# Gated expert values made during attention, the down projection as seven products of blocks, and a transposed result

## The chip, the cores and the metric

The kernel runs on one core of one Trainium2 chip. The metric is the time of one execution on the device in microseconds (us); lower is better. The median of three runs of the kernel before is 1683.87 us (1683.67 to 1683.97).

## The reference

One input x of S = 2048 tokens and D = 512 goes through softmax attention (H = 32 heads of 16) and through a gated expert (F = 1792), and a gate per token mixes the two:

```python
g = sigmoid((x * gate_w).sum(-1, keepdims=True))
q, k, v = split(x @ wqkv)                     # 32 heads of 16
a = softmax(q @ k.T * 16 ** -0.5) @ v @ wo    # per head, heads joined before wo
h = sigmoid(x @ w_gate) * (x @ w_up)          # 2048 x 1792
b = h @ w_down
return g * a + (1 - g) * b
```

Everything is float32. The kernel keeps that precision on TensorE by writing each operand as a high part and a low rest (fp32r) and adding three matmuls for one product: high x high, high x low, low x high.

## The kernel before

**Words used here.** PE is TensorE, ACT ScalarE, DVE VectorE, POOL GpSimd; SP's queue starts the DMAs. P = 128 rows; a chunk c is 512 of the 2048 tokens; f counts the 14 row blocks of 128 of the hidden size. `split` (ends in L104) makes the high part by a copy on ACT (L101) and the low rest by a subtraction on DVE or POOL. Work on PE, ACT, DVE and POOL runs in the order in which the code emits it; SP's DMAs are put where what they need is ready.

**Attention** is a loop over 256 periods `k`, each for two blocks of keys. In a period PE makes eight scores for the maxima (L292; DVE reduces each, L294), eight scores for the exponentials (L679; ACT, L681), twelve half-height matmuls of other dense work (L162: the gate and up projections, the projections of queries and keys, then the first heads), and at its end sixteen matmuls of the values (L842), whose 128x512 sum ACT copies (`part`, L847) and POOL adds (`sum`, L859). The string `STEADY` gives the order of these, `spot` the bank of each. After every 32 steps of keys, in each eighth period (k mod 8 = 4), DVE transposes the maxima (L298, L300) and POOL splits them (L319). The word `turn` is a token: an empty POOL instruction that waits for PE's half-height matmuls on one half of the array, and that the matmuls of the other half wait for. It stands in POOL's row among POOL's other work.

POOL's work comes from queues (`later`, `turnover`, `slow`), from which `work(2.0)` and `work(2.6)` take entries twice per period by an estimated cost: the sums (`sum`), the combinations of the dense products (`chain`, `had`, `side`, L542), and the splits of weights (`ca`, `cb`, L139 and L136). In periods 75 to 122 DVE also computes the gate's logits (L829, sixteen in all). From period 245 on (`FREE`) no maxima are left and the order `LAST` is used.

The gate and up projections go to `gu_d` in DRAM, as gate and up before the sigmoid. In the last 16 periods the hidden values of the first two pairs of blocks are made (`hidden_early`: exponentials on ACT, L768, and reciprocals on DVE, L776).

**The tail** has 28 rounds (c, two blocks f), each of 24 down matmuls (L1034), with a chunk's four token blocks in four banks. For each round ahead of PE a 512 KB load of gate and up comes in, ACT applies the sigmoid (L759), DVE multiplies (L760), ACT and DVE split the product (L101, L104). ACT and POOL split the rest of `w_down` and `wo` in the first rounds. The heads' values are multiplied by the reciprocal denominators (L987, from `rec_d`), split, and multiplied by `wo` (L149) in eight places between the rounds; `finish` (L1002, L1006) scales with the gate, a column of one number per token, adds, and stores rows of tokens. The denominators' reciprocals are L800.

Of the kernel before, what the change touches and what calls it, by code (L numbers as in the profile page):

```python
# [25 lines left out]
P = 128  # L26
KT = D // P
# [12 lines left out]
EARLY = 5  # L40
# [6 lines left out]
def gated_mix(ctx, tc, x, xT, wqk, wv, wo, w_gate, w_up, w_down, gate_w, out):  # L47
# [26 lines left out]
    hp_d = dram.tile([2 * EARLY, P, D], F32, name="hp_d")  # L74
# [122 lines left out]
    xes = ExitStack()  # L197
    xp = xes.enter_context(tc.tile_pool(name="xp", bufs=1))
# [123 lines left out]
    wd = []  # L322

# [64 lines left out]
    def filling():  # L388
# [5 lines left out]
        jobs += [("heads", 0), ("down", 0)]  # L394
# [5 lines left out]
        def raws(kind, n):  # L400
# [9 lines left out]
            if kind == "down":  # L410
                return [raw_weights(w_down[f * P:(f + 1) * P, :], [P, D], f"wd{f}") for f in range(2)]
# [8 lines left out]
        def weights(kind, n, loaded):  # L420
# [4 lines left out]
            if kind in ("heads", "down"):  # L425
                return [split_weights(r) for r in loaded]
# [49 lines left out]
        def sums_of(kind, n, ws):  # L476
# [29 lines left out]
            elif kind == "heads":  # L506
                for u in range(EARLY):
                    while split_of[u] in later:
                        later.pop(0)[1]()
                    oh, ol = [t for t in first_heads(u)][:2]  # L510
                    for a in range(2):
                        cols = slice(a * P, (a + 1) * P)
                        run = Sum(bankd(), [((oh[:, k, cols], ol[:, k, cols]), ws[k]) for k in range(2)])
                        yield run
                        sp.dma_start(hp_d[2 * u + a], out_of(run, f"hp{u}_{a}"))
# [54 lines left out]
        for job, nxt in zip(jobs, jobs[1:]):  # L570
            kind, n = job
            coming = None
            for at, run in enumerate(sums_of(kind, n, ws)):
# [13 lines left out]
                if kind == "heads" and at in (2, 4, 6):  # L587
                    if at == 2:
                        first_heads_load(4)
                    first_heads_split(at // 2 + 1)  # L590
                if at == ask[kind][0]:
                    coming = raws(*nxt)
                if at == ask[kind][1]:
                    new = weights(*nxt, coming)
                    end = turnover[-1]
# [9 lines left out]
        wd.extend(ws)  # L605
# [106 lines left out]
    chunks = [(c, f) for c in range(NC) for f in range(0, NF, 2)]  # L712

    def hidden_load(c, f):
        gu = big(f"gul{c}_{f}").rearrange("p (a f s) -> p a f s", a=2, f=2)
        for a in range(2):
            sp.dma_start(gu[:, a], gu_d[a, f:f + 2, :, c * 512:(c + 1) * 512].rearrange("f p s -> p f s"))
        return gu

    def late_raw(src, r):  # L720
        if src is w_down and r in (6, 8):
            raw = [keep.tile([P, D], F32, name=f"late{r + a}", tag="er", bufs=6) for a in range(2)]
            for a in range(2):
                sp.dma_start(raw[a], src[(r + a) * P:(r + a + 1) * P, :])
            return raw
        raw = keep.tile([P, 2, D], F32, name=f"late{r}", tag="ev", bufs=2)
        sp.dma_start(raw, src[r * P:(r + 2) * P, :].rearrange("(k p) d -> p k d", p=P))
        return raw

    def down_late(f, raw):  # L730
        if f < 6:
            th, tl, bufs = ("wh", "wl", 4) if f < 4 else ("sum", "part", 2)
            for a in range(2):
                if f + a == 5:
                    th = tl = "wr"
                h = keep.tile([P, D], F32R, name=f"wd{f + a}h", tag=th, bufs=bufs)
                l = keep.tile([P, D], F32R, name=f"wd{f + a}l", tag=tl, bufs=bufs)
                split(h, l, raw[:, a, :], act, pool)
                wd.append((h, l))
        else:  # L740
            fs = slice(f - 6, f - 4)
            if f < 10:
                for a in range(2):
                    split(wd_h[:, f - 6 + a, :], wd_l[:, f - 6 + a, :], raw[a], act, pool)
# [157 lines left out]
    for k in range(NPER):  # L902
# [27 lines left out]
        if k == NPER - 1:  # L930
            break
# [157 lines left out]
```

## Time and profile before

| | |
|---|---|
| median of the runs | 1683.87 us |
| span of the profiled execution | 1682.4 us |
| PE busy | 1677.3 us (100%) |
| DVE busy | 1451.8 us (86%) |
| ACT busy | 1362.8 us (81%) |
| POOL busy | 941.9 us (56%) |
| bytes moved by DMA | 254.20 MB |
| first down matmul to the last | 1493.87 to 1678.5 us |

The profile is of one execution. "Busy" counts the time in which an engine had an instruction running. A row of an engine in order of time reads: start, duration (both us), engine, line, operation, output <- input, shape, number of instructions, and in brackets how long the engine sat idle before it and what released it. A group's row has the sum of the busy time and the mean of one in ns, then idle time by releaser. A row with "x16" covers sixteen instructions that follow each other.

### The profile page before, as it was taken

The numbers are of one execution on the slowest core, as the hardware profiler recorded it, in microseconds if no ns is written. First come the engines' busy times: TensorE is split into PE (matmuls) and PEld (weight loads), VectorE is DVE, ScalarE is ACT, GpSimd is POOL, SyncE is SP. The second block draws the span as 40 slices with busy tenths as digits, with TensorE's granted clock in tenths as the row PEclk, the third lists the DMA queues.
The fourth block names the chain that finished last, engine by engine and source line by source line (L and its number), as shares of the span: only waits on it lengthen the run. The fifth ranks groups of instructions, "written<-read, shape, count | busy, mean of one in ns | idle before, by whom it ended". The sixth has DMA issues, their size and how long they took to land.

```text
span 1682.4 us, 34644 instructions
## 1 busy us (share of the span) xinstructions
PE 1677.3 (100%) x12485; PEld 1063.3 (63%) x12485; DVE 1451.8 (86%) x2347; ACT 1362.8 (81%) x2659; POOL 941.9 (56%) x922
## 2 busy tenths in 40 slices
PE   9999999999999999999999999999999999999999
PEld 7766566665656565656565666656565656568887
DVE  7988888888889999999888888888999888887853
ACT  4188898989888898889898989898898989983431
POOL 1034476547666666666666767676766667653110
PEclk9999999999999999999999999999999999999999
DMA  7511457356565564566635353534353534368861
GB/s 247 140 48 59 128 175 210 134 164 209 143 199 133 167 153 157 159 165 184 166 102 146 102 145 108 134 103 133 107 137 104 133 115 153 128 205 277 294 211 70
DMA packets 143788, 254.20 MB, mean 151 GB/s; under 512 B 24256, under 2 KB 36544, under 8 KB 140736
## 3 DMA queue, kind: packets, MB, share of 16 engines
q1 hardware_dynamic: 136000, 237.30, 47.1%
q10 hardware_dynamic: 7616, 14.68, 2.8%
q8 instruction: 98, 1.61, 0.4%
q14 instruction: 74, 0.61, 0.2%
HBM read 149.42 MB, written 102.50 MB: 150 GB/s over the span
## 4 chain that ended last, share of the span: by engine, by line
PE 97%; DVE 3%; issue 0%; DVEq 0%
PE dn L162 29%; PE sm L842 27%; PE sm L292 15%; PE sm L1034 5%; PE st L679 5%; PE sm L679 4%; PE st L292 2%; DVE stat L294 2%; PE dn L1034 2%; PE st L1034 2%; PE st L643 1%; PE st L149 1%; PE sm L149 1%; PE st L162 1%; PE st L842 1%; PE st L85 0%
## 5 line engine op out<-in xcount | busy, mean ns | idle before, releaser
L294 DVE TENSOR_REDUCE stat<-sm 128x1 f32<-128x512 f32 x1313 | 847.9, 681 | 140.4 <-PE sm L679 126.5
L681 ACT ACTIVATE p<-st 128x512 f32<-128x512 f32 x1019 | 619.2, 655 | 1.1 <-PE st L679 1.1
L681 ACT ACTIVATE p<-sm 128x512 f32<-128x512 f32 x1027 | 611.1, 632 | 0.5 <-PE sm L679 0.2
L292 PE MATMUL sm<-ks,qs 48*128 48x512 f32 x1313 | 522.6, 436 | 0.3
L842 PE MATMUL sm<-p,v 128*17 128x512 f32 x4016 | 480.0, 595 | 0.0
L294 DVE TENSOR_REDUCE stat<-st 128x1 f32<-128x512 f32 x735 | 479.5, 680 | 0.1
L679 PE MATMUL sm<-qs,ks 64*128 64x512 f32 x1027 | 427.6, 419 | 0.0
L679 PE MATMUL st<-qs,ks 64*128 64x512 f32 x1019 | 426.5, 419 | 0.0
L292 PEld LDWEIGHTS sm<-ks,qs 48*128 48x128 f32 x1313 | 239.6, 184 | 259.3 <-DVE stat L294 212.3
L859 POOL TENSOR_TENSOR sum<-sum,part 128x512 f32<-128x512 f32 x224 | 288.6, 1288 | 135.7 <-PE sm L679 118.4
L292 PE MATMUL st<-ks,qs 48*128 48x512 f32 x735 | 290.5, 395 | 0.0
L842 PEld LDWEIGHTS sm<-p,v 128*17 128x17 f32 x4016 | 93.2, 97 | 224.2 <-issue 155.1
L847 ACT ACTIVATE part<-sm 128x512 f32<-128x512 f32 x214 | 128.2, 599 | 124.4 <-issue 83.8
L542 POOL TENSOR_TENSOR chain<-chain,chain 128x512 f32<-128x512 f32 x96 | 124.1, 1292 | 156.3 <-PE sm L679 139.5
L679 PEld LDWEIGHTS st<-qs,ks 64*128 64x128 f32 x1019 | 187.7, 184 | 30.0 <-issue 3.4
L679 PEld LDWEIGHTS sm<-qs,ks 64*128 64x128 f32 x1027 | 189.6, 185 | 9.9 <-issue 5.1
L542 POOL TENSOR_TENSOR had<-chain,had 128x512 f32<-128x512 f32 x96 | 123.5, 1287 | 39.3 <-PE sm L679 20.3
L292 PEld LDWEIGHTS st<-ks,qs 48*128 48x128 f32 x735 | 137.3, 187 | 2.1 <-ACT v L662 0.3
L607 ACT ACTIVATE chain<-dn 128x512 f32<-128x512 f32 x128 | 89.2, 697 | 0.0
L542 POOL TENSOR_TENSOR side<-side,side 128x512 f32<-128x512 f32 x32 | 41.3, 1292 | 76.5 <-PE sm L679 66.1
L104 POOL TENSOR_TENSOR ol<-ot,oh 128x512 fp32r<-128x512 f32 (+1 forms) x8 | 14.7, 1840 | 102.5 <-ACT oh L101 102.5
L319 POOL CAST mhl<-mt 128x32 fp32r<-128x32 f32 x32 | 7.5, 236 | 102.7 <-DVE mt L300 102.7
(913 smaller groups left out, 3253.5 us busy)
## 6 DMA issues: line engine op xcount, KB each, us to landing
gul<-gu_d SPq DMA_DIRECT2D x56, 512.0 KB
had<-gu_d SPq DMA_DIRECT2D x84, 256.0 KB
gu_d<-had SPq DMA_DIRECT2D x84, 256.0 KB
gu_d<-side SPq DMA_DIRECT2D x56, 256.0 KB
pv_d<-sum SPq DMA_DIRECT2D x32, 256.0 KB
qs<-q_d SPq DMA_DIRECT2D x30, 256.0 KB
ks<-k_d SPq DMA_DIRECT2D x30, 256.0 KB
gu_d<-far SPq DMA_DIRECT2D x28, 256.0 KB
```

What stands on the lines that cost most here:

```text
L149: pe.matmul(o, a, b, start=(i == 0), stop=(i == len(ops) - 1))
L162: mm = pe.matmul(self.o, a[rows], b[rows], start=(self.n == 0), stop=(self.n == 2 * len(self.ops) - 1))
L292: pe.matmul(t, qs[r:r + KM, qt * P:(qt + 1) * P], ks[r:r + KM, g * 512:(g + 1) * 512], start=True, stop=True)
L294: dve.tensor_reduce(stat[half][:, b, qt % 8, g:g + 1], t, axis=AX.X, op=ALU.max)
L542: pool.tensor_tensor(to, u, w, ALU.add)
L607: leave = lambda e, o: act.activation(e, o, AF.Copy)
L679: pe.matmul(o, ks[r:r + KR, (kt + a) * P:(kt + a + 1) * P], qs[r:r + KR, q0:q0 + 512], start=True, stop=True)
L681: act.activation(pt[:, 2 * a + c, :], o, AF.Exp, scale=DH ** -0.5)
L842: pe.matmul(o[32 * c:32 * c + VW, :], v[:, 2 * k % 16 + a, h * VW:(h + 1) * VW], pts[c // 2][:, 2 * a + c % 2, :], start=(a == 0), stop=(a ...
L847: act.activation(e, o, AF.Copy)
L859: pool.tensor_tensor(s, s, e, ALU.add)
L1034: pe.matmul(down[t], a, b, start=(f == 0 and m == 0), stop=(f == NF - 2 and m == 5))
```

## The change

**Hidden values.** They are made during attention now. In periods 143 to 249 thirteen "quads" go through: four blocks of a block row pair (i, i + 7) and a chunk pair (c, c + 2). Each of the four has two loads of 256 KB (gate and up), a tanh in two pieces of 128x256 on ACT, one per period, ahead of the values matmuls, and one scalar_tensor_tensor (tanh + 1) * up on DVE, 128x512, right behind the values matmuls of every second period. POOL forms four differences of the four blocks (`quad_steps`, L737), through the queue `later`. The seven operands of each quad, 128x512, are stored to `op_d`. The fourteenth quad is made in the tail (`last_quad`). The factor 1/2 of sigmoid(g) = (tanh(g/2) + 1)/2 goes into the gate's factor g0.

**Down projection.** Hidden values and `w_down` are cut into two by two blocks (of tokens and of F against F and output columns), and each half of the tokens takes seven products in place of eight (A11, A12, A22, S1, S2, S4, S3), each of 7 blocks f x 2 x 3 matmuls. The weights are the stationary operand, so the result is transposed: 128 output columns x 512 tokens. `op_load` and `op_split` bring one operand each, four ahead of PE by the code; `after` adds the products up on DVE. The weight blocks for the first two products are split on DVE in the last periods (`first_weights`); those for the other five are made in the tail by seven calls of `w_split`, with four POOL additions each. The operand tiles of the first four come from tag w, the others from three tiles of two.

**Gate and heads.** The gate's factor is a row now: g0 and g1 go through `g_d` in DRAM and come back broadcast over partitions; g1 is multiplied into the reciprocal denominators (one more DVE operation for each), g0 into the sums on POOL (`scaled`). The early heads are ten transposed half sums (`hp_d`), added on POOL (`plus`). The denominators' reciprocals stand in periods 144 to 215 and, for the second half, at operands 18 to 36 of the tail. The host transposes the result. A scratch size for DMA is set to 1024.

On DVE, at the transposition of maxima in a period with k mod 8 = 4, the rows of before (`stat` are the maxima, `mpad` and `mt` the transposition):

```order
L294 TENSOR_REDUCE stat_0_11201<-sm_71 128x1
L294 TENSOR_REDUCE stat_0_11201<-sm_72 128x1 x2
L294 TENSOR_REDUCE stat_0_11201<-st_65 128x1
L294 TENSOR_REDUCE stat_0_11201<-st_67 128x1
L294 TENSOR_REDUCE stat_0_11201<-sm_72 128x1
```

and of after, in a period with the transposition and in the second one behind it:

```order
L294 TENSOR_REDUCE stat_0_11247<-sm_72 128x1
L298 TENSOR_REDUCE mpad_95<-stat_0_11247 128x16
L300 STREAM_TRANSPOSE mt_0_11793<-mpad_95 128x32
L745 SCALAR_TENSOR_TENSOR hu_11605<-hg_11533,hu_11605 128x512
L294 TENSOR_REDUCE stat_1_11824<-sm_72 128x1
...
L294 TENSOR_REDUCE stat_1_11824<-sm_72 128x1
L745 SCALAR_TENSOR_TENSOR hu_11744<-hg_11674,hu_11744 128x512
L294 TENSOR_REDUCE stat_1_11824<-sm_72 128x1
```

The multiplication (`hu` is up, `hg` the tanh) stands between the last reduction before the values and the first one behind them, and behind the transposition where there is one; in the first listing, a period of before without a transposition, reductions follow each other.

On POOL, some 20 periods into the new work, at the weights `cb(0, 2)`; before:

```order
L139 CAST cb(0, 2)h<-chain_9r 128x512
L136 TENSOR_TENSOR cb(0, 2)l<-chain_9r,cb(0, 2)h 128x512
L542 TENSOR_TENSOR chain_01_11519<-chain_01_11519,chain_00_11449 128x512
L542 TENSOR_TENSOR had_00_11381<-chain_01_11519,had_00_11381 128x512
L859 TENSOR_TENSOR sum_1_11467<-sum_1_11467,part_11534 128x512
```

and after:

```order
L140 CAST cb(0, 2)h<-chain_9r 128x512
L540 TENSOR_TENSOR chain_12_11945<-chain_12_11945,chain_11_11874 128x512
L540 TENSOR_TENSOR had_12_11876<-chain_12_11945,had_12_11876 128x512
L137 TENSOR_TENSOR cb(0, 2)l<-chain_9r,cb(0, 2)h 128x512
L900 TENSOR_TENSOR sum_1_11529<-sum_1_11529,part_11958 128x512
L737 TENSOR_TENSOR hu_11744<-hu_11744,hu_11605 128x512
L540 TENSOR_TENSOR chain_13_12014<-chain_13_12014,chain_12_11945 128x512
L900 TENSOR_TENSOR sum_1_11529<-sum_1_11529,part_12035 128x512
L737 TENSOR_TENSOR hu_11458<-hu_11744,hu_11458 128x512
```

The second half of the weights' split has moved a period on, behind `had`, and the differences (`hu`, L737) stand behind the sums.

On ACT, the first rows behind the last exponentials; after (`op` are the operands loaded, `late` the weights' raw block, whose five copies go to `wohl`, `xh`, `S3h`, `S2h` and `xh`):

```order
L102 ACTIVATE ops_18773<-op_18713 128x512
L102 ACTIVATE wohl<-late_18753 128x256
L102 ACTIVATE xh<-late_18753 128x256
L102 ACTIVATE S3h<-late_18753 128x256
L102 ACTIVATE S2h<-late_18753 128x256
L102 ACTIVATE xh<-late_18753 128x256
L102 ACTIVATE ops_18773<-op_18715 128x512
L102 ACTIVATE ops_18816<-op_18717 128x512
L102 ACTIVATE wohl<-late_18755 128x256
```

where before had sigmoids and copies of double width, independent of each other:

```order
L101 ACTIVATE hl_18368<-gul_10_18184 128x1024
L101 ACTIVATE wd_h<-late_18199 128x1024
L759 ACTIVATE gul_0_18287<-gul_0_18287 128x1024
L101 ACTIVATE hl_18402<-gul_12_18243 128x1024
L101 ACTIVATE wd_h<-late_18254 128x1024
```

The operand behind a block's five copies comes on only when they are through.

The diff, cut to what the prediction speaks of:

```diff
-    def hidden(m):
-        gu = loaded[m]
-        act.activation(gu[:, 0], gu[:, 0], AF.Sigmoid)
-        dve.tensor_tensor(gu[:, 1], gu[:, 0], gu[:, 1], ALU.mult)
...
+    def hid_tanh(g, cols=slice(0, 512)):
+        act.activation(g[:, cols], g[:, cols], AF.Tanh, scale=0.5)
...
+    def quad_steps(i, c, u):
+        def minus(a, b, to, n):
+            def step(engine):
+                engine.tensor_tensor(u[to], u[a], u[b], ALU.subtract)
+                hid_out(c, n, i, u[to])
+            return step
+        return [minus(1, 0, 1, 3), minus(2, 1, 2, 4), minus(2, 0, 0, 6), minus(3, 2, 3, 2)]
...
+    def hid_mult(i, c, j, g, u):
+        dve.scalar_tensor_tensor(u, g, 1.0, u, op0=ALU.add, op1=ALU.mult)
+        if j in OUT:
+            hid_out(c, OUT[j], i, u)
...
+            k = k0 + 2 * j
+            plans(k, "load", lambda j=j, f=f, ci=ci: load(0, j, f, ci))
+            plans(k + 1, "load", lambda j=j, f=f, ci=ci: load(1, j, f, ci))
+            for a in range(2):
+                plans(k + 1 + a, "act", lambda j=j, a=a: hid_tanh(g[j], slice(a * 256, (a + 1) * 256)))
+            plans(k + 3, "dve", lambda j=j: hid_mult(i, c, j, g[j], u[j]))
+        for off, step in zip((6, 8, 9, 10), quad_steps(i, c, u)):
+            plans(k0 + off, "load", lambda step=step: later.append((1.3, lambda: step(pool))))
...
+            plan_quad(i, c, 143 + 16 * i + 8 * c)
...
+        dve.tensor_tensor(den[rows, :], den[rows, :], gwb[rows, :], ALU.mult)
         sp.dma_start(rec_d[rows, :], den[rows, :])
...
         spot[:] = [seven[SUMS]]
         values(k)
+        planned(k, "dve")
...
+    def w_split(f):
+        raw = late.pop(("raw", f))
+        (a11, a21), (a12, a22) = [(raw[:, a, :256], raw[:, a, 256:]) for a in range(2)]
+        split(*late["A22"][f], a22, act, dve)
+        pool.tensor_tensor(a22, a21, a22, ALU.add)
+        split(*S1[f], a22, act, dve)
+        pool.tensor_tensor(a21, a11, a21, ALU.subtract)
+        split(*late["S3"][f], a21, act, dve)
+        pool.tensor_tensor(a11, a22, a11, ALU.subtract)
+        split(*late["S2"][f], a11, act, dve)
+        pool.tensor_tensor(a12, a12, a11, ALU.subtract)
+        split(*S4[f], a12, act, dve)
...
+    def scaled(c, t, a):
+        pool.tensor_tensor(a, a, late["g0"][c], ALU.mult)
+        acc[c, t] = a
+        plus(c, t)
...
+    for f, (m, at) in enumerate(((0, 2), (0, 4), (3, 7), (5, 9), (8, 12), (10, 14), (13, 17))):
+        step_at(m, lambda f=f: w_load(f))
+        step_at(at, lambda f=f: w_split(f))
...
+    for half in range(2):
+        for n, name in enumerate(PRODUCTS):
+            o = two_banks()
+            for fs in ((0, 1), (2, 3), (4, 5, 6)):
+                for j in range(2):
+                    for f in fs:
+                        w = late[name] if late else A11
+                        h, l = ops[m + f]
+                        cols = slice(j * P, (j + 1) * P)
+                        for i, (a, b) in enumerate(((0, h), (0, l), (1, h))):
+                            pe.matmul(o[j], w[f][a][:, cols], b, start=(f == 0 and i == 0),
+                                      stop=(f == HF - 1 and i == 2))
+                if m == 0 and fs[0] == 0:
+                    values(NPER - 1)
+                    flush(later)
+                    late_tiles()
+                for f in fs:
+                    op_split(m + f + 4)
+                    op_load(m + f + 9)
+                    for step in steps.pop(m + f, ()):
+                        step()
+                    ops.pop(m + f)
+            m += HF
+            after(half, n, o)
+        for c, t, ks in HEADS[half]:
+            heads_out(c, t, ks)
```

451 lines of the change are left out of this document (242 added, 209 removed).

## The prediction

> **What bounds the kernel now.** I read the page first (busy shares, then the chain of waits that ended last), then the values matmuls of attention in order of time, then DVE and POOL around them, and last the stretches of the tail.
>
> ```profile
> span 1682.4 us, 34644 instructions
> PE 1677.3 (100%) x12485; PEld 1063.3 (63%) x12485; DVE 1451.8 (86%) x2347; ACT 1362.8 (81%) x2659; POOL 941.9 (56%) x922
> PE 97%; DVE 3%; issue 0%; DVEq 0%
> ```
>
> PE is busy all the time, and 97% of the chain is PE. The median of the runs, 1683.87 us, is 1.47 us above the span; I take that as unchanged and add it at the end. A measurement of this kernel can tell about 0.2% (3.4 us) from no change.
>
> Attention is a row of periods, each ending in 16 values matmuls (L842). Their starts, in order of time:
>
> ```profile
> 513.72 1.91 PE L842 MATMUL sm<-p,v 128*17 128x512 f32 x16
> 519.29 1.91 PE L842 MATMUL sm<-p,v 128*17 128x512 f32 x16
> 525.29 1.91 PE L842 MATMUL sm<-p,v 128*17 128x512 f32 x16
> 530.86 1.91 PE L842 MATMUL sm<-p,v 128*17 128x512 f32 x16
> ```
>
> A period is 5.57 us when nothing disturbs it; the middle one is 6.00. So PE's full row hides that something else can lengthen it. What that is shows on DVE behind the values of another period (start 905.39), with POOL's row below:
>
> ```profile
> 905.79 1.28 DVE L294 TENSOR_REDUCE stat<-sm 128x1 f32<-128x512 f32 x2
> 907.77 0.69 DVE L294 TENSOR_REDUCE stat<-sm 128x1 f32<-128x512 f32 x1 [0.70 <-PE sm L679]
> ```
> ```profile
> 906.40 1.27 POOL L859 TENSOR_TENSOR sum<-sum,part 128x512 f32<-128x512 f32 x1
> ```
>
> DVE has one gap per period, 0.70 us, between the last maximum before the values and the first one after; it opens at about 906.99 (reductions follow each other every 0.60), and POOL's sum runs through it until 907.67. The rest of the period is reductions that PE's maxima wait for. This gap is where the change puts its multiplications.
>
> The tail, from the first down matmul at 1493.87 to 1678.5, as stretches (us, then busy time and count of PE, PEld, DVE, ACT, POOL, clock, DMA share, GB/s), and a piece of the chain there:
>
> ```profile
> 1493.90:1678.50 184.60, 184.60 (x821) 151.08 (x820) 120.86 (x110) 69.18 (x78) 44.29 (x22) 1.00 0.69 228
> 1500.00:1550.00 50.00, 50.00 (x222) 41.42 (x221) 42.47 (x29) 25.56 (x29) 28.07 (x14) 1.00 0.91 302
> ```
> ```profile
> 1500.34 1.36 PE sm L1034 x6
> ```
>
> Six matmuls take 1.36 us, 0.2267 each, and PE never waits there: 672 down and 132 heads matmuls are 182.3 us, the last values 1.84, together 184.1 of 184.6.
>
> **The change part by part.** *Fewer matmuls.* The down projection goes from 672 to 2 x 7 x 7 x 6 = 588 matmuls of the same size; 84 x 0.2267 = **19.0 us less on PE**, all of it on the path as long as PE is fed. The heads' matmuls keep their number.
>
> *Multiplications in the gap.* 52 scalar-tensor-tensor operations (L745, 128x512, two inputs in SBUF) stand on DVE behind the values of every second period, 50 of them before the last 11 periods: k mod 8 = 2 (13), 4 (13), 6 (12), 0 (12). Nothing like them is in those periods before, but the logits' operation (L829) is of the same size with two SBUF inputs, in the same gap. Two of them with the reduction that follows, and POOL beside the first:
>
> ```profile
> 520.90 1.27 DVE L829 CUSTOM_DVE_ANT_0 xn<-xn,gwb 128x512 f32<-128x512 f32 x1
> 522.10 0.68 DVE L294 TENSOR_REDUCE stat<-sm 128x1 f32<-128x512 f32 x1
> ...
> 554.75 0.68 DVE L829 CUSTOM_DVE_ANT_0 xn<-xn,gwb 128x512 f32<-128x512 f32 x1
> 555.54 0.69 DVE L294 TENSOR_REDUCE stat<-sm 128x1 f32<-128x512 f32 x1
> ```
> ```profile
> 520.90 0.73 POOL L448 TENSOR_TENSOR side_8r<-side_8r 128x256 f32<-128x256 f32 x1
> ```
>
> With POOL idle (554.75) it takes 0.68 and the next reduction comes 0.79 after it began: no loss. Beside a POOL operation it takes 1.27, the next reduction stands 0.47 behind POOL's end at 521.63, and the period is the one of 6.00: +0.42. In k mod 8 = 2 and 6 POOL's sum lies where the row of 906.40 shows it, until 907.67; 0.47 behind that is 908.14, against 907.77: +0.37 each, 25 x 0.37 = 9.2 us. [...]
>
> In k mod 8 = 4 the maxima are transposed in the gap, and the operation comes behind that:
>
> ```profile
> 560.84 0.65 DVE L829 CUSTOM_DVE_ANT_0 xn<-xn,gwb 128x512 f32<-128x512 f32 x1
> ```
> ```profile
> 558.73 1.91 PE L842 MATMUL sm<-p,v 128*17 128x512 f32 x16
> 564.61 1.91 PE L842 MATMUL sm<-p,v 128*17 128x512 f32 x16
> ```
>
> It took 0.65, undisturbed, and still that period is 5.88, +0.30: 13 x 0.30 = 3.9 us. In k mod 8 = 0 POOL's work before is
>
> ```profile
> 937.19 1.29 POOL L542 TENSOR_TENSOR chain<-chain,chain 128x512 f32<-128x512 f32 x1 [1.70 <-PE sm L679]
> 938.43 1.29 POOL L859 TENSOR_TENSOR sum<-sum,part 128x512 f32<-128x512 f32 x1
> ```
>
> and then one of the new subtractions (1.29). The period ahead of it has one subtraction and a cast's second half more, which pushes this row by about 0.78: the subtraction then starts 1.59 behind the values, and DVE's gap opens 1.60 behind them. It is a tie: POOL first costs 1.29 - 0.30, about 1.0; DVE first costs nothing. I take half for the 10 periods in which the subtraction stands there: 5 us (0 to 10).
>
> Two multiplications for the denominators, 0.6 us. In period 239 POOL gets four operations of 1.29, a sum of 1.27 and a cast of about 0.6 between two tokens that dense matmuls wait for: 7.0 against 5.57, 1.5 us late. In the last 11 periods ACT is the bound and gets three tanh pieces more, priced by exponentials of that shape:
>
> ```profile
> L768 ACT ACTIVATE gul<-gul 128x256 f32<-128x256 f32 x8 | 3.2, 492 | 0.0
> ```
>
> 1.5 us. (The other 101 pieces lie in periods where ACT's slack hides them, as it hid two of these per period in before.) The stage sums to 9.2 + 3.9 + 5 + 0.6 + 1.5 + 1.5 = **21.7 us**; bounds 8 (POOL is always the one to wait, the tie falls to DVE) and 27 (the tie falls to POOL).
>
> *Weights split in the tail.* Seven blocks are made while the first 22 operands run, each with five ACT copies, five DVE subtractions and four POOL additions of 128x256, in a chain through three engines. On ACT and DVE the operands' splits are queued behind them, and PE waits for those. Durations, and how DVE and POOL get on in the tail:
>
> ```profile
> L759 ACT ACTIVATE gul<-gul 128x1024 f32<-128x1024 f32 x26 | 27.3, 1048 | 11.3 <-DMA gul<-gu_d 9.4 <-issue 1.6
> L104 POOL TENSOR_TENSOR wd_l<-late,wd_h 128x1024 fp32r<-128x1024 f32 x2 | 6.8, 3424 | 1.0 <-ACT wd_h L101 1.0
> L987 DVE TENSOR_TENSOR ot<-ot,rb 128x512 f32<-128x512 f32 x5 | 3.5, 691 | 12.2 <-DMA rb<-rec_d 12.2
> L101 ACT ACTIVATE wd_h<-late 128x512 fp32r<-128x512 f32 x4 | 2.3, 620 | 1.2 <-PE sm L1034 1.2
> ```
> ```profile
> 1516.91 1.21 DVE L760 TENSOR_TENSOR gul<-gul 128x1024 f32<-128x1024 f32 x1
> 1518.04 3.43 DVE L104 TENSOR_TENSOR hl<-gul,hl 128x1024 fp32r<-128x1024 f32 x1
> ```
>
> ACT: 1048 and 620 ns give 0.40 for 256 columns. DVE: 1.21 and 0.69 give 0.43. POOL: 0.73 (row of 520.90). The rows of 3.43 and 3424 ns, where the two lay side by side, show that they take turns: 3.43 is 1.21 and a whole POOL operation. One block is then 4 x 0.73 + 5 x 0.43 = 5.05 us; side by side, as one copy, one subtraction, four additions and one copy, it would be 4.15. Say T1 is the first product matmul. The blocks can start once v's tile is free, after two operands and the last values: 2.72 + 1.84 = 4.6. Then 7 x 5.05 = 35.4, ACT's copies for 16 operands queued between them, 16 x 0.62 = 9.9, and POOL's rows for the first finished product (two times a factor and a partial sum, 5.2, some 4 of it in the way): operand 22 is ready at T1 + 54. PE would want it at 1.84 + 22 x 1.36 = 31.8. **Stall 22 us**, bounds 12 (4.15 per block, and the rest hidden) and 28.
>
> From operand 34 to 48 PE has 15 x 1.36 = 20.4 us. DVE has 15 operand subtractions and 12 operations on the heads at 0.69 (18.6), 8 product additions (5.5), and parts of the last quad and the denominators (3), 27 us, while POOL takes turns with it for 12 operations of 1.29. Six operands made ahead, as many as the change has buffers for, cover 8 us at most. I take **11**, bounds 0 and 22. At the end of each half, POOL's factors and partial sums (six of 1.29) come before the heads' additions that free PE's two banks; **5**, bounds 0 and 8. The tail is **38 us**, bounds 12 and 58.
>
> *At nothing:* the sigmoid's table load and the factors' rows, on ACT and DVE beside running matmuls; the early heads keep their matmuls; the transposed output ends in one addition and one store as before.
>
> Sum: 1682.4 - 19.0 + 21.7 + 38 + 1.47 = 1724.6, say **1724 us**. From the bounds: -19 + 8 + 12 = +1, 1685, and -19 + 27 + 58 = +66, 1750.
>
> **The rivals.** *Only the tail costs.* POOL, not DVE, waits in the gap: for it speaks that a logits operation which began first lost nothing; against it that POOL's sum begins 0.6 before the gap in half the periods. 1683.9 - 19 + 38 = 1703 us; chance 0.16.
>
> *Only the gap costs.* The blocks are made in time, because splits for several operands are ahead when the products begin. Against it: the three-engine chain has no slack in the queue. 1683.9 - 19 + 21.7 = 1686.6, with the stage's bounds 1673 to 1692; chance 0.08, of which a quarter is faster and half no change.
>
> *Faster.* Both preparations are hidden and PE decides alone: in the gap the two engines miss each other, and the chain for a block runs ahead of PE. Its place is operand 22; it decides when a block and its share of the operands (2.3 of them, 1.4 us) take less than PE's 2.3 x 1.36 = 3.1 us or the lead makes up for it. PE's full row in the tail of before speaks for it, with DVE at 121 of 184.6 us; against it that a block needs 4.15 at best. 1683.9 - 19 = 1665 us; chance 0.10.
>
> *Transfers decide as well.* DMA stands at a share of 0.91 in 1500 to 1550, and the operands' loads add to it; if they come late on top, 20 to 40 us more, some 1755 to 1765. Other work waits first, so 0.06.
>
> **How the numbers follow.** The forecast with both costs has 0.60, with the range 1700 to 1750. The whole range, 1685 to 1750, leaves out the faster case, half of the gap-only case and the late transfers, 0.20. Faster: 0.10 and a quarter of 0.08, 0.12. Same: half of 0.08, 0.04. Slower: 0.84.
>
> **What would show it.** In the profile after: 588 product matmuls; periods from k = 146 on of 5.9 to 6.0 in the even places and 5.57 in the odd ones; L745 at over 1.0 us in k mod 8 = 2 and 6 and at 0.68 in 4; PE idle between the first product and operand 22 waiting for DVE's or ACT's splits, some 20 us; POOL and DVE operations of 128x256 that end one behind the other. I'm wrong if the periods stay at 5.57, or if PE has no gap in the first 40 us of the tail.

## The result, and the profile after

The changed kernel takes **1816.76 us** (median of four runs, 1814.07 to 1817.36), the kernel before 1683.92 us beside it (1683.67 to 1684.09): 1.0784 times as long, 95% interval 1.0769 to 1.0799. It was forecast slower, at 1724 us with an upper end of 1750; it is slower by three times as much. Its profiled execution has a span of 1815.6 us, 133.2 more than before. The page of it:

```profile
span 1815.6 us, 35561 instructions
PE 1721.3 (95%) x12401; PEld 1056.3 (58%) x12401; DVE 1545.9 (85%) x2528; ACT 1409.6 (78%) x2833; POOL 1048.6 (58%) x1013
PE 76%; DVE 8%; DMA 7%; POOL 4%; issue 3%; ACT 2%; SPq 0%; POOLq 0%; DVEq 0%; ACTq 0%
```

PE has fewer matmuls than before and is busy longer, 1721 us against 1677: they have become slower (the mean granted clock of TensorE is 0.971, before it was 1.000). PE's share of the chain has gone from 97% to 76%, and transfers, which were not on it at all, hold 7%.

Where the 133.2 us lie follows from the starts of the values matmuls in both traces, and the end:

| stretch | before, us | after, us | more |
|---|---|---|---|
| start to period 143 | | | 0.8 |
| periods 143 to 243 | 563.2 | 636.1 | 72.9 |
| periods 244 to 254 | 45.0 | 53.0 | 8.0 |
| last values matmuls to the end | 185.6 | 237.1 | 51.5 |

The forecast had 20.2 (18.7 for the multiplications and the denominators, 1.5 for period 239), 1.5 and 19.0 (38 taken less 19 saved) for the last three rows. Attention is where it failed most. Taking each period less the same period of before, and sorting by k mod 16:

| k mod 16 | more in all, us | each |
|---|---|---|
| 1 | 40.0 | 7.4 to 8.5 in 161, 177, 193, 209 and 225, else 0 |
| 2 | 11.1 | 0.3 to 1.6, 4.2 in 242 |
| 0 and 8 | 7.9 | 0.9 in most |
| 4 and 12 | 4.8 | 0.4 |
| 6 and 14 | 4.1 | 0.35 |
| 10 | 2.0 | 0 or 0.6 to 0.7 |
| all others | 3.0 | 0, few up to 1.3 |

The rows at 0, 4, 6, 8, 12 and 14 are the forecast's gap. The row at 1 was not in it. POOL's row in period 161, in order of time:

```profile
991.50 1.29 POOL L540 TENSOR_TENSOR had<-chain,had 128x512 f32<-128x512 f32 x1 [2.07 <-PE sm L678]
1000.76 1.26 POOL L737 TENSOR_TENSOR hu<-hu,hu 128x512 f32<-128x512 f32 x1 [7.97 <-DMA op_d<-hu]
```

The last subtraction of a quad stands still for 7.97 us. It writes its difference over the fourth hidden block, and that block's store to `op_d` still reads it. SP's queue issued two such stores from 992.37 on (count and time of both in one row), and the chain of waits has the second one's way to DRAM, from 993.48 on, as a piece of 7.15 us:

```profile
992.37 1.43 SPq L727 DMA_DIRECT2D op_d<-hu  x2
```
```profile
993.48 7.15 DMA op_d<-hu
```

DMA's busy share (next to last number; then GB/s) from 990 to 1000 goes with that: the loads of the next pair of heads (L251 and L252, issued from 986.1 to 990.2) and this store are in it together.

```profile
990.00:1000.00 10.00, 7.05 (x51) 4.04 (x50) 8.90 (x15) 7.07 (x15) 1.29 (x1) 1.00 1.00 271
```

In period 249, without the loads of a pair and at a share of 0.77 in 1545 to 1553, such a store is on its way for 3.40 us:

```profile
1549.99 3.40 DMA op_d<-hu
```

POOL waits a sixth time there, 8.60 us, because SP's queue issued that store only at 1549.99; PE stands 3.43 us behind it. In all other quads the wait for the store is 1.81 us at most.

Back to period 161: behind the subtraction in POOL's row stands the token that PE's half-height matmuls wait for, and PE says so, first in the list of what it waited for in 900 to 1500 (us in total, times, longest), then in its own row:

```profile
PE dn L163 <- POOLq L174: 31.3, 5, 6.8
```
```profile
996.21 0.39 PE L163 MATMUL dn<-xl,ca(0, 2)h 64*128 64x512 f32 x1
996.45 0.39 PE L163 MATMUL dn<-xh,ca(0, 2)l 64*128 64x512 f32 x1
1003.62 0.79 PE L163 MATMUL dn<-xh,ca(0, 2)h 64*128 64x512 f32 x1 [6.05 <-POOLq L174]
...
1005.06 0.62 PE L163 MATMUL dn<-xh,ca(0, 2)h 64*128 64x512 f32 x1
1005.49 0.62 PE L163 MATMUL dn<-xl,ca(0, 2)h 64*128 64x512 f32 x1
```

Ahead of the wait a matmul of this line follows the other by 0.24 us, behind it by 0.43: PE also comes back slow. That is in the 40 us, and in the 11 of the period behind.

The tail, as stretches with PE's granted clock (first of the last three numbers):

```profile
1600.00:1610.00 10.00, 6.01 (x21) 3.90 (x20) 7.50 (x13) 5.72 (x13) 4.27 (x6) 0.95 0.59 175
1620.00:1630.00 10.00, 3.78 (x9) 2.70 (x10) 4.86 (x9) 3.95 (x9) 6.30 (x8) 0.66 0.54 166
1660.00:1670.00 10.00, 6.11 (x21) 3.66 (x19) 9.79 (x15) 2.96 (x6) 2.87 (x2) 0.85 0.73 239
```

Where before had 44 matmuls in 10 us, these have 9 to 21. T1, the first product matmul, is at 1575.55; the first matmul of operand 22 starts 57.3 us behind it, that of operand 34 at 78.9, the first half's heads start at 120.0, operand 49 at 140.9, the last heads at 215.1, and the end is at 240.0. At PE's pace (0.2267 us per matmul, 1.84 for the last values) these would lie at 31.1, 46.7, 68.5, 82.1, 148.7 and some 169.

### The profile page after: what moved, and what is told of

Same layout as the page of the kernel before. It is cut to its first block, busy times and chain, and to the rows that moved or that the text cites. A ratio compares the mean times of both kernels' runs of the same rounds, so it can differ in the third digit from the quotient of the medians.

```text
span 1815.6 us, 35561 instructions
## 1 busy us (share of the span) xinstructions
PE 1721.3 (95%) x12401; PEld 1056.3 (58%) x12401; DVE 1545.9 (85%) x2528; ACT 1409.6 (78%) x2833; POOL 1048.6 (58%) x1013
## 4 chain that ended last, share of the span: by engine, by line
PE 76%; DVE 8%; DMA 7%; POOL 4%; issue 3%; ACT 2%; SPq 0%; POOLq 0%; DVEq 0%; ACTq 0%
PE dn L163 25%; PE sm L883 23%; PE sm L292 13%; DVE stat L294 4%; PE st L678 4%; PE sm L678 4%; DMA op_d<-hu 2%; PE st L292 2%; PE sm L1175 2%; PE st L150 1%; DVE ops L105 1%; PE st L642 1%; ACT p L680 1%; DVE hu L745 1%; DMA ks<-k_d 1%
## 5 line engine op out<-in xcount | busy, mean ns | idle before, releaser
L680 ACT ACTIVATE p<-st 128x512 f32<-128x512 f32 x1019 | 611.6, 644 | 6.4 <-PE st L678 6.3
L883 PE MATMUL sm<-p,v 128*17 128x512 f32 x4016 | 487.5, 603 | 0.0
L737 POOL TENSOR_TENSOR hu<-hu,hu 128x512 f32<-128x512 f32 x52 | 67.3, 1294 | 61.6 <-DMA op_d<-hu 57.5
L102 ACT ACTIVATE ops<-op 128x512 fp32r<-128x512 f32 x94 | 54.8, 626 | 60.3 <-PE sm L1175 24.2
L105 DVE TENSOR_TENSOR ops<-op,ops 128x512 fp32r<-128x512 f32 x94 | 76.8, 847 | 19.2 <-ACT ops L102 18.2
```

The source lines that it names most:

```text
L105: return lo.tensor_tensor(l, src, h.bitcast(F32), ALU.subtract)
L680: act.activation(pt[:, 2 * a + c, :], o, AF.Exp, scale=DH ** -0.5)
L737: engine.tensor_tensor(u[to], u[a], u[b], ALU.subtract)
L883: pe.matmul(o[32 * c:32 * c + VW, :], v[:, 2 * k % 16 + a, h * VW:(h + 1) * VW], pts[c // 2][:, 2 * a + c % 2, :], start=(a == 0), stop=(a ...
```

## The experiments

Every kernel was measured once, beside a run of the kernel before, which took 1684.2 to 1684.5 us in each; effects under some 3 us are not read from the totals but from the traces. "Tail" below is from the first product matmul to the end; three kernels with the same tail code had 240.0, 237.6 and 238.5, so a difference under 3 us says little there. Attention moves too: adds_dve, adds_first and apart have late_difference's attention code and 3 to 5 us more in periods 143 to 243, most of it in 238 to 243.

**late_difference**: the waiting subtraction goes two periods on.

```diff
-        for off, step in zip((6, 8, 9, 10), quad_steps(i, c, u)):
+        for off, step in zip((6, 8, 9, 12), quad_steps(i, c, u)):
```

> The changed kernel with the last subtraction of each quad queued two periods later (offset 12 in place of 10); nothing is left out. Theory of the store: in periods 161, 177, 193, 209 and 225 that subtraction overwrites a tile whose store is queued behind the loads of the next pair of heads, POOL waits some 8 us for it, and the token that PE's half-height matmuls wait for stands behind. Two periods later the store has landed: the five periods fall from 13 to 14 us to about 5.6, the slow ones behind them from 6.9 to about 6, and the whole is about 50 us shorter, some 1767 us. Rival, POOL's load: POOL simply has too much to do around the loads of a pair, and the wait shows up where the queue happens to stand: the five long periods stay, or move two periods on, and the time stays within 10 us of 1816.

Measured: **1768.76 us**, 48.0 less. The row k mod 16 = 1 falls from 40.0 to 0.2 us, the whole of periods 143 to 243 from 72.9 to 31.4, the last periods from 8.0 to 3.7, where the wait of period 249 is gone too; the other 2.4 us are the tail's, and within what equal tails differ by. DMA is as full at that place as in the kernel it comes from, and POOL goes on working:

```profile
990.00:1000.00 10.00, 9.83 (x77) 5.60 (x77) 9.75 (x18) 8.56 (x18) 8.60 (x9) 1.00 1.00 279
```
```profile
PE dn L163 <- POOLq L174: 1.3, 1, 1.3
```

POOL's load is the same, so the rival falls: it is the wait for the store, and its place ahead of the token, that cost some 46 of these 48 us.

**mult_before**: the kernel before, with the multiplications alone.

```diff
         values(k)
+        if 146 <= k < 245 and k % 2 == 0:
+            dve.scalar_tensor_tensor(gwb, gwb, 1.0, gwb, op0=ALU.mult, op1=ALU.max)
```

> The kernel before, with 50 additional multiplications (scalar_tensor_tensor 128x512, two inputs in SBUF, on a tile that nobody needs any more) behind the values of every second period from 146 to 244; the result is the same. Theory of the gap: the collision alone makes periods longer, without any of the change's other work: +0.3 to 0.4 us in k mod 8 = 2, 4 and 6, nothing or little in k mod 8 = 0, where POOL's sum has ended and the subtraction of the change is not there; about 38 x 0.36 = 14 us in all, some 1698 us. Rival: the longer periods of the changed kernel come from its transfers or POOL's added work, and DVE's gap takes the operation: within 2 us of 1684.

Measured: **1701.15 us**, 17.0 more than before; periods 143 to 243 are 18.3 longer. The starts of its values matmuls, k = 146 to 150:

```profile
903.91 1.91 PE L842 MATMUL sm<-p,v 128*17 128x512 f32 x16
909.85 1.91 PE L842 MATMUL sm<-p,v 128*17 128x512 f32 x16
915.42 1.91 PE L842 MATMUL sm<-p,v 128*17 128x512 f32 x16
921.34 1.91 PE L842 MATMUL sm<-p,v 128*17 128x512 f32 x16
926.91 1.91 PE L842 MATMUL sm<-p,v 128*17 128x512 f32 x16
```

5.94, 5.57, 5.92, 5.57: each of these periods with a multiplication is some 0.35 longer, each without is as before. In k mod 8 = 0 it cost nothing in eight of twelve, where POOL's sum is over, and 0.2 to 1.1 in the other four. So the gap's cost stands by itself. Per period it is the forecast's; the sum is above the 13.1 (9.2 and 3.9) that the forecast had without POOL's subtraction beside it, by those four periods and five of k mod 8 = 2 and 6 with 0.7 to 1.1.

**gap_free** and **gap_free_2**: late_difference, with POOL held behind the multiplication and the second multiplication of a quad a period later.

```diff
+        gap = 146 <= k < FREE and (k, "dve") in plan
+        if gap:
+            work_to(2.7)
+        else:
+            work(2.6)
...
         planned(k, "dve")
+        if gap:
+            hold = pool.nop()
+            tc.add_manual_dep(hold.ins, mult[0].ins.name, SYNC, reason="POOL behind the multiplication")
+            work_to(4.6)
```

`work_to` takes POOL's entries up to that total since the last token. In the table of the quad the second multiplication is at k0 + 6 in place of k0 + 5. A load and a tanh of the fourth block and the first subtraction also move a period on, and a third of the denominators' reciprocals goes from k mod 8 = 5 to 7.

> The kernel late_difference with two more edits; nothing is left out. In periods with a multiplication POOL does at most two operations before it, waits for it, and does its sum behind it; and the second multiplication of each quad moves one period on, out of the periods in which the maxima are transposed. Theory of the gap: a multiplication that nothing runs beside costs nothing (0.68 us in a gap of 0.70), so the some 0.3 to 0.4 us in k mod 8 = 2, 4, 6 and the 0.9 in 0 go: 15 to 20 us less than 1768.8, some 1751 us, with periods of 5.6. Rival: POOL has no room to wait, its tokens come late, and PE's half-height matmuls lose what the gap wins: within 5 us of 1769.

Measured: 3184.95 us, with periods of 10.37 us. This number says nothing of the edit: PE was slow from the first instruction on, ahead of all that the edit touches. The nine warm-up matmuls took 5.70 us (first row; second row: the same nine in late_difference), and those behind them came every 0.62 us, against 0.23. Why is not known.

```profile
0.92 5.70 PE L86 MATMUL st<-warm 128*128 128x512 f32 x9 [0.92 <-DVE warm L82]
```
```profile
0.92 4.21 PE L86 MATMUL st<-warm 128*128 128x512 f32 x9 [0.92 <-DVE warm L82]
```

> The same kernel as gap_free: late_difference with POOL's sum held behind the multiplication and the second multiplication of each quad moved out of the periods with a transposition. In the first run of it PE made a matmul in 0.62 us from the very first on, long before anything that was edited, so its time tells nothing of the edit. Expected as before: theory of the gap, 15 to 20 us less than 1768.8, some 1751 us, with periods of 5.6; rival, POOL's tokens come late, within 5 us of 1769.

Measured: **1761.65 us**, 7.1 less than late_difference, not 15 to 20. In the gap the theory holds. DVE in period 146, and POOL beside it:

```profile
907.06 0.68 DVE L755 SCALAR_TENSOR_TENSOR hu<-hg,hu 128x512 f32<-128x512 f32 x1
907.85 0.69 DVE L304 TENSOR_REDUCE stat<-sm 128x1 f32<-128x512 f32 x1
```
```profile
905.18 1.28 POOL L550 TENSOR_TENSOR had<-chain,had 128x512 f32<-128x512 f32 x1
907.88 1.29 POOL L910 TENSOR_TENSOR sum<-sum,part 128x512 f32<-128x512 f32 x1 [1.42 <-ACT hg L734]
```

The next reduction comes 2.38 behind the values (905.47), as in the kernel before, and most multiplications are shorter (ns, least/median/most; gap_free_2, then the changed kernel):

```profile
L755 DVE SCALAR_TENSOR_TENSOR hu<-hg,hu x52: 669/682/1742, 907.1 to 1496.4; 128x512 f32<-128x512 f32 x52
```
```profile
L745 DVE SCALAR_TENSOR_TENSOR hu<-hg,hu x52: 660/1208/1774, 907.7 to 1546.3; 128x512 f32<-128x512 f32 x52
```

By class, k mod 16 = 4, 6, 10 and 12 cost 0.0 us in all, 9.6 in late_difference; 0 and 8 cost 3.7 in place of 9.0. But k mod 16 = 2 rises from 5.7 to 13.8. In 162, 178 and 210 POOL waited for a load of its own, its `had` slid into the gap, and the sum was held behind both. 6.9 of it are in 242, where PE stands 4.99 us for ACT; that was not taken apart. So the rival has a part of it: POOL has room to wait in most periods, not in those behind the loads of a pair.

**no_adds**: the tail's weight blocks without POOL's 28 additions.

```diff
-        pool.tensor_tensor(a22, a21, a22, ALU.add)
...
-        pool.tensor_tensor(a21, a11, a21, ALU.subtract)
...
-        pool.tensor_tensor(a11, a22, a11, ALU.subtract)
...
-        pool.tensor_tensor(a12, a12, a11, ALU.subtract)
```

> The changed kernel without the 28 POOL additions that form the weight blocks in the tail (the blocks S1 to S4 are then copies of the raw parts; all copies and splits stay). Theory of the chain: the copies, subtractions and additions of a block follow each other over three engines, about 5 us per block, and operands queue behind; without the additions a block is five copies and five subtractions side by side, about 2.2 us, operand 22 is ready at about T1 + 35 in place of T1 + 57, and the tail is 20 to 25 us shorter, some 1793 us. Rival, transfers: the first operands and raw blocks land too late, whatever is done with them: the stall before operand 22 stays over 20 us and the time within 5 us of 1816.

Measured: **1800.41 us**; the tail is 224.3 us, 15.7 shorter, and operand 22 starts at T1 + 41.5 in place of 57.3. Attention is as in the changed kernel (71.2 against 72.9). So of the 26 us that operand 22 is late, 16 are the additions, less than the 20 to 25 that the theory had. The other 10 were not tried apart: DVE's first split of a block starts 8.6 us behind T1 in this kernel too, where the forecast had 4.6, and ACT waits four times for a raw block, 5.1 us in all. POOL's row with them, two blocks of seven in the changed kernel:

```profile
1603.99 0.73 POOL L1014 TENSOR_TENSOR late<-late 128x256 f32<-128x256 f32 x1 [2.71 <-DVE wohl L105]
1604.80 0.74 POOL L1016 TENSOR_TENSOR late<-late 128x256 f32<-128x256 f32 x1
1605.62 0.80 POOL L1018 TENSOR_TENSOR late<-late 128x256 f32<-128x256 f32 x1
1606.50 0.79 POOL L1020 TENSOR_TENSOR late<-late 128x256 f32<-128x256 f32 x1
1610.60 0.73 POOL L1014 TENSOR_TENSOR late<-late 128x256 f32<-128x256 f32 x1 [3.31 <-DVE wohl L105]
```

These two blocks are 6.6 us apart, operands' copies included; the forecast's 5.05 and 2.3 x 0.62 make 6.5. Over all seven it is 7.3: DVE's first splits of the blocks start from T1 + 8.5 to T1 + 52.5.

**adds_dve** and **adds_first**: the additions on DVE, between the splits, or ahead of them. Both kernels carry the edit of late_difference as well, though the first expectation names the changed kernel: they are to be compared with late_difference (tail 237.6).

```diff
         split(*late["A22"][f], a22, act, dve)
-        pool.tensor_tensor(a22, a21, a22, ALU.add)
+        dve.tensor_tensor(a22, a21, a22, ALU.add)
+        dve.tensor_tensor(a21, a11, a21, ALU.subtract)
+        dve.tensor_tensor(a11, a22, a11, ALU.subtract)
+        dve.tensor_tensor(a12, a12, a11, ALU.subtract)
         split(*S1[f], a22, act, dve)
-        pool.tensor_tensor(a21, a11, a21, ALU.subtract)
         split(*late["S3"][f], a21, act, dve)
```

> The changed kernel with the 28 additions of the weight blocks on DVE in place of POOL; nothing is left out. Theory of the chain: a block's nine steps on DVE, 0.36 to 0.43 us each, and two copies are 4.0 to 4.7 us where four additions of 0.75 to 0.8 on POOL, alternating with DVE, and their handovers take 5.05 and more; operand 22 is ready 4 to 8 us earlier and the tail, 240 us from the first product to the end, is that much shorter. Rival, DVE is the bound of the whole tail: the additions are 10 us more on it, and the tail stays or gets up to 10 us longer.

Measured: **1779.03 us**, 10.3 more than late_difference, 5 of them in attention, which the edit leaves alone. The tail is 242.9, and operand 22 is at T1 + 62.2: both 5 us worse. DVE's row shows handovers as well as load: each split of a sum waits for ACT's copy, and the next addition waits in the row behind it. All 28 of these splits wait ahead of operand 22, 13.6 us in all. The time is the one that the rival, DVE's load, had; the next run tells the two apart.

```profile
1565.06 0.42 DVE L1014 TENSOR_TENSOR late<-late 128x256 f32<-128x256 f32 x1
1565.97 0.43 DVE L105 TENSOR_TENSOR xl<-late,xh 128x256 fp32r<-128x256 f32 x1 [0.48 <-ACT xh L102]
1566.32 0.42 DVE L1016 TENSOR_TENSOR late<-late 128x256 f32<-128x256 f32 x1
1567.22 0.42 DVE L105 TENSOR_TENSOR S3l<-late,S3h 128x256 fp32r<-128x256 f32 x1 [0.48 <-ACT S3h L102]
```

> The kernel late_difference (1768.8 us) with a block's four additions on DVE, one behind the other, and the four splits of the sums behind them; nothing is left out. In adds_dve each addition stood between two splits, so DVE waited for ACT's copy five times per block; that kernel carried late_difference's edit too and is compared with it: +10 us, 5 of them in the tail. Theory of the chain: what counts is how often a block passes from engine to engine; now it passes twice, a block takes about 3.8 us in place of 5.05, and operand 22 is ready about 9 to 13 us earlier than with late_difference (57 us behind the first product), the tail 5 to 13 us shorter. Rival, DVE's load: its row is 10 us longer by the additions whatever their order; operand 22 comes no earlier than 55 us and the tail stays within 3 us of late_difference's or gets longer.

Measured: **1764.89 us**, 3.9 less than late_difference; the tail is 229.7, 7.9 shorter, and operand 22 starts at T1 + 49.0, 8.3 earlier (attention took 3 us more than in late_difference, in k = 238 and 242). DVE's splits of the sums now follow each other, and none of the 28 waits:

```profile
1564.45 0.42 DVE L105 TENSOR_TENSOR xl<-late,xh 128x256 fp32r<-128x256 f32 x1
1564.79 0.42 DVE L105 TENSOR_TENSOR S3l<-late,S3h 128x256 fp32r<-128x256 f32 x1
```

The same instructions in another order, 13 us apart at operand 22, as much as the waits that are gone: in adds_dve the handovers set the pace there, not DVE's work.

**keep_warm**: PE is given 100 matmuls more, into a free bank.

```diff
+                if 2 <= m + fs[0] < 22:
+                    for _ in range(5 * len(fs)):
+                        pe.matmul(banks[1], A11[0][0][:, :P], h, start=True, stop=True)
```

> The changed kernel with five more matmuls per operand (100 in all, into an unused bank, 22.7 us of PE at full clock) behind operands 2 to 21 of the tail; nothing is left out. Theory of waiting: PE idles in that stretch anyway, 25 us of it, so the added matmuls lie in the waits and the first 22 operands take no more than 5 us longer. If the lower granted clock (0.66 to 0.95 there) is itself on the path, the added work keeps the clock at 1.00 and the stretch gets shorter by up to 5 us. Rival: PE's own slow matmuls set the pace there: 15 to 22 us longer.

Measured: **1810.63 us**. Operand 22 starts at T1 + 60.1, 2.8 later, with 22.7 us of matmuls added; the tail is 237.1. The waits were long enough to hold them. In that stretch the mean granted clock rises from 0.88 to 0.97, and nothing is won by it: the slow matmuls lay beside waits.

**heads_lead**, **no_recips** and **apart**: the tail behind operand 22. A unit is a 128x512 block of the heads' values with its denominators. heads_lead loads the units earlier and uses them later, on the changed kernel; no_recips leaves the second half's reciprocals out, on late_difference; apart has adds_first, heads_lead and the low part of a unit one operand later.

```diff
-            step_at(base + 2 * n, lambda c=c, k=k: heads_load(c, k))
-            step_at(base + 2 * n + 3, lambda c=c, k=k, n=n: heads_split(c, k, n > 3))
+            step_at(base + (-3, -1, 3, 5, 7, 9)[n], lambda c=c, k=k: heads_load(c, k))
+            step_at(base + (2, 4, 7, 9, 11, 13)[n], lambda c=c, k=k, n=n: heads_split(c, k, n > 3))
```

> The changed kernel with the loads of the heads' units one to three operands earlier, and the multiplication that waits for them four to five operands behind the load in place of three; nothing is left out. Theory of late transfers: in both halves DVE's row stops at a unit whose denominators have not landed (3.95 us at one), and the operands' splits behind it make PE wait; the waits before matmuls 276 to 283 and 571 to 576, 9 and 4 us, become small and the tail is 8 to 12 us shorter. Rival: DVE and POOL are full there anyway: the tail changes by less than 3 us.

```diff
-        for a in range(n):
+        for a in range(n if r0 == 0 else 0):
             cols = slice(a * 512 // n, (a + 1) * 512 // n)
             dve.reciprocal(den[rows, cols], den[rows, cols])
```

> The changed kernel without the sixteen reciprocals of the second half of the denominators that stand at operands 18 to 36 of the tail, 8.7 us of DVE; the denominators of those heads are used as they are. Theory of DVE's load: from operand 22 to 38 DVE is busy 9.5 to 9.8 of each 10 us, so the tail gets 6 to 9 us shorter. Rival, transfers: operands land late, and DVE only looks full: the tail changes by less than 2 us.

```diff
-        split(h, l, ot, act, dve)
-        unit[c, k] = h, l
+        act.activation(h, ot, AF.Copy)
+        unit[c, k] = h, l, ot
+
+    def heads_low(c, k):
+        h, l, ot = unit[c, k]
+        dve.tensor_tensor(l, ot, h.bitcast(F32), ALU.subtract)
+        unit[c, k] = h, l
```

> The kernel adds_first (1764.9 us, tail 229.7 us from the first product to the end) with the heads' loads one to three operands earlier as in heads_lead, and with the low part of each heads' unit one operand behind its multiplication, so that DVE does not stand and wait for ACT's copy; nothing is left out. Theory: from operand 34 to the last head DVE's row stops 0.70 us at each of six units for ACT and up to 4 us for a load, and both halves have these stops; without them the tail is 6 to 12 us shorter, some 1756 us. Rival: DVE's work, and POOL's that it alternates with, fill that stretch; the stops only move, and the tail changes by less than 3 us.

Measured: heads_lead 1811.06 us, tail 236.6 against 240.0; no_recips 1768.09, tail 233.6 against 237.6; apart 1767.35, tail 231.7 against 229.7 of adds_first. The first two win 3 to 4 us, between theory and rival, and near what equal tails differ by. The third is a miss: the wait that it took away came back one row on. DVE in the changed kernel, and in apart:

```profile
1669.97 0.69 DVE L1068 TENSOR_TENSOR ot<-ot,rb 128x512 f32<-128x512 f32 x1
1671.35 0.69 DVE L105 TENSOR_TENSOR ol<-ot,oh 128x512 fp32r<-128x512 f32 x1 [0.70 <-ACT oh L102]
```
```profile
1619.74 0.69 DVE L1068 TENSOR_TENSOR ot<-ot,rb 128x512 f32<-128x512 f32 x1
1621.65 0.69 DVE L105 TENSOR_TENSOR ops<-op,ops 128x512 fp32r<-128x512 f32 x1 [1.22 <-ACT ops L102]
1622.26 1.76 DVE L1079 TENSOR_TENSOR ol<-ot,oh 128x512 fp32r<-128x512 f32 x1
```

ACT copies the unit first and then the operand, so DVE now waits 1.22 for the operand. From operand 22 to the end all these kernels need 176 to 183 us, where PE's pace would make it 138.

**together**: apart with the edits of gap_free.

> The kernel apart with the two edits of gap_free (POOL's sum behind the multiplication, no multiplication at a transposition); nothing is left out. If the costs are separate, attention is as in gap_free_2 (7 to 8 us shorter than without those edits) and the tail as in apart, some 1748 us; all that remains above 1665 us is then some 25 us in attention, 4 in its last periods and 50 in the tail, so no mixture of these edits comes below the kernel before. If the costs hide each other, it is within 3 us of apart.

Measured: **1759.21 us**, 8.1 less than apart: periods 143 to 243 are 26.3 longer than before (36.4 in apart), the last periods 4.0, the tail is 232.5. The costs are separate; the expected 1748 counted on 1756 for apart, which took 1767. This is the best mixture tried, still 75 us above the kernel before.

## Why the prediction was wrong

**Held: PE's work.** 588 product matmuls run in the trace, 84 fewer, worth 19.0 us at 0.2267 each; none of it is seen, since PE waits (94 us of the span without work, 5 before).

**Held: the gap, as a mechanism and per period.** The forecast was 18.7 us for the multiplications with the denominators' two. In late_difference, without the store's wait, the three classes have some 23 (without 238 and 242). That mult_before made 18.3 is in part luck, since it lacks the subtraction to which the forecast gave 5. By class: 0.28 to 0.40 in most periods for 0.37 and 0.30. The row of the first one in the changed kernel is the working's own case, the reduction 0.48 behind the end of POOL's sum (907.10 to 908.38) where 0.47 was read:

```profile
907.74 1.19 DVE L745 SCALAR_TENSOR_TENSOR hu<-hg,hu 128x512 f32<-128x512 f32 x1
908.86 0.68 DVE L294 TENSOR_REDUCE stat<-sm 128x1 f32<-128x512 f32 x1
```

The tie in k mod 8 = 0 fell to POOL, 0.9 where half of 1.0 had been taken. In mult_before 20 of the 25 periods with k mod 8 = 2 or 6 have 0.29 to 0.38, where 0.37 had been taken.

**Failed: the transfers of a step that was added.** The working priced the 52 subtractions by their 1.29 us on POOL and by where they stand at DVE's gap. It did not ask what each waits for. The fourth writes over a block whose store is under way, and in five quads the store shares the queue with the loads of a pair. The forecast's "transfers decide as well" looked at the tail alone and at bandwidth; what decided was one late landing, on an engine whose row holds PE's token. That is some 46 us of the 93 by which the forecast was short, as late_difference shows.

**Failed: what a wait costs PE.** The sum took a wait at its length. Behind each of the five waits PE ran at half pace for 4.6 to 6.0 us. At the first, the granted clock was 0.50 from 1001.5 to 1008.2, that is from 4 us after the start of the wait of 6.05 to nearly 5 us behind its end, with 0.43 us per matmul against 0.24; over the five it fell to 0.50 between 1.4 and 4.8 us after the start of the wait. How much of the 46 us this is was not tried apart; k mod 16 = 2 went from 11.1 to 5.7 with the waits gone. In the tail keep_warm shows that a clock of 0.97 in place of 0.88 wins nothing in the first 22 operands.

**Right in kind, short in size: the tail.** Operand 22 was put at T1 + 54 and came at 57.3: the chain through three engines is the forecast's, and no_adds and adds_first show it. But 38 us were taken for the whole tail and some 70 are there: 51.5 more and the 19 saved. Against PE's pace operand 22 is 26 late (22 taken), operands 22 to 34 add 6, those from 34 to the first half's heads 19 (11 taken), those heads 7 (5 taken), the second half 8 and the last heads and the end 5 (nothing taken). The steps at fault are those that were given nothing, the operands between 22 and 34 and the second half with its end, whose units the forecast did not look at (19 us), and the term for operands 34 to 48, taken at 11 and measured at 19. What holds operands 22 to 49 is not settled. DVE's row is full at places (9.79 of 10 us in 1660 to 1670), stops for ACT and for loads at others, and alternates with POOL (operations of 0.69 take 1.70 and 1.76 at 1664.62 and 1687.66, beside POOL's of 1.3 to 1.7); taking away one of these moved 3 to 4 us at most, or none.

**Short: the last periods.** 3.0 forecast with period 239; 3.7 remain in 244 to 254 without the store's wait, and 7.9 in 238, 239 and 242, where POOL has the early heads to make as well. What is late there was not taken apart.

## What to carry to other kernels

An operation that is added to an engine's row brings its waits as well as its length, here up to 8.60 us of wait for 1.28 of work: for one that writes in place, ask which transfer still reads the tile, what else is in that queue then, and what stands behind it in the row. A token in that row passes the wait on to the engine that was the bound, here 31.3 us of PE's in 900 to 1500; two periods of distance left 1.3, for one number changed. A slot between two of an engine's operations is not free for being empty: in mult_before the same multiplication cost nothing in most periods in which POOL's sum was over, and some 0.35 us beside that sum or behind a transposition.

## What the runs showed of the hardware

The same four additions and five splits of a block took operand 22 to T1 + 62.2 or 49.0 by their order in DVE's row alone: DVE, which works through its row in order, stood some 0.48 us for each copy on ACT, 28 times, and in the row sorted so that the additions cover the copies it stood for none of them.

Reading a share of 1.00 on DMA does not by itself mean that PE waits: the kernel with the edit of one number has the same 1.00 in 990 to 1000, at 279 GB/s against 271, and PE is busy for 9.83 of those 10 us in place of 7.05.
